# Half a pair earlier: the order of the gate sums in the output stage of an attention and feed-forward kernel

## The chip, the core and the metric

The kernel runs on one core of a Trainium2 chip. The metric is the device time of one execution in microseconds (us), as the median of several runs. A core has five engines that run side by side, each through its own instructions in a fixed order: TensorE (PE in the profile, with its weight loads as PEld), VectorE (DVE), ScalarE (ACT), GpSimd (POOL) and SyncE (SP), which here issues the transfers. An engine waits at an instruction until the semaphores that it names have been reached, and everything behind it on that engine waits as well.

## The reference

The inputs are q, k, v of shape (8, 8, 576, 64), w_in of (512, 2048) and w_out of (2048, 512). What is computed, cut to what matters:

```
attn_out = attention(q, k, v)       # 4 heads see the last 32 positions, 4 heads every 32nd one
x = attn_out.transpose(0, 2, 1, 3).reshape(4608, 512)
h = x @ w_in                        # 4608 x 2048
g = h * cos(h)
out = g @ w_out                     # 4608 x 512
```

## The kernel before

The program has two stages. In the first, which ends 486 us into the span, the attention and h = x @ w_in are made batch by batch, and h goes to a scratch array in memory. The second, the output stage, makes g and g @ w_out. It is the one that the change touches.

**Blocks and pairs.** The output stage goes through 18 blocks of 256 tokens, s0 to s17, and in each through 8 pairs, f0 to f7; a pair is 256 of the 2048 columns of h. A tile (s, f) of h is 128 partitions by 512 numbers. Products are made with numbers split in two: a high part that the fast matrix format holds, and the rest, the low part. A pair needs the high part of its gate against both parts of w_out and then the low part against the high part of w_out (`pair`, line 697). A plain pair takes 12 matmuls of 512 columns: 8 with the gate's high part, 4 with the low part. In blocks 1 to 16 the pairs f1, f3 and f5 are made with seven products in place of eight (a 2 by 2 Strassen scheme): 21 matmuls of 256 columns, 14 with the high part and 7 with the low part. For this their gates are summed first, so their tile has 896 numbers a partition rather than 512.

**The gate of one tile** (`gate`, line 631) is made in steps, each a piece of a generator:

- the load of h (`h_in`, line 634, SyncE's queue, 5 buffers);
- ScalarE turns h into a whole number of turns (line 641, into `r`, 3 buffers), and VectorE takes these off (line 642, a scalar_tensor_tensor that reads `r` and `h_in`, both in SBUF); below these two are called the count and the reduction;
- ScalarE takes the sine (`wave`, line 645, in PSUM, 3 buffers), and VectorE multiplies by h (line 652 for plain pairs, line 659 for pairs with seven products; one input is in PSUM);
- for pairs with seven products GpSimd makes the sums in three instructions (lines 660, 661, 664);
- ScalarE casts the high part (line 175), and the rest is taken off for the low part (line 176): on GpSimd, for f2 and f4 on VectorE. The buffers of `g_hi` and `g_lo` are three each.

**What sets the order.** Before each pair, `ahead` (line 674) begins one more step for the tiles that lie 2, 3, 4 and 6 pairs ahead (LEADS). From this a scheduler makes the fixed order of each engine, with estimates of its own; it also chooses which of the three buffers of `r` a tile takes. Which buffer is taken matters in the prediction: the count of f1 writes the `r` that the low part of the block before's f6 has read last.

**Around the pairs.** The outputs of a block stand in four PSUM tiles, and a fifth is free (`seats`, line 686). The tile "most" of a block is the tile "lower" of the block before it, so the first matmul into "most", the eleventh in pair f1, waits until VectorE has written that block's first half out (line 745). For the shared sums of the seven products, ScalarE copies a bank after f5 (line 730), and VectorE adds three times (lines 731, 733, 736).

**The last tiles of w_out.** Six of the 16 tiles of w_out are loaded and split only when the output stage begins (line 899, LATE). The cast is by ScalarE for three and by VectorE for the other three, and GpSimd takes the low part of all six.

Of the kernel before, what the change touches and what calls it, by code (L numbers as in the profile page):

```python
# [26 lines left out]
P = 128  # L27
# [52 lines left out]
NTB = NTOK // TB  # L80
SEVEN = (1, 3, 5)

LEADS = (6, 4, 3, 2)
AHEAD = tuple(PER_BATCH - n for n in (20, 17, 13, 10, 7, 3))

BY_VECTOR = (2, 4)
# [11 lines left out]
def attention_cos_ffn(ctx, tc, qkl, vl, qkvs, w_in, w_out, eye, eye16, mask_l0, mask_l, mask_s, out):  # L98
# [74 lines left out]

    def split(x, hi, lo, cast=nc.scalar.copy, rest=nc.gpsimd):
        with_product(cast(out=hi, in_=x))  # L175
        rest.tensor_tensor(out=lo, in0=x, in1=hi.bitcast(F32), op=ALU.subtract)  # L176

    wi, whole = [], []

# [398 lines left out]
        nc.sync.dma_start(out=w_all[n], in_=t)  # L578
        yield

    def output_weights(room, n, cast):
        both = room()
        t = wp.tile([P, 2, 2, 2 * P], F32R, name="w", bufs=2 * NF).rearrange("p l m n -> p l (m n)")
        nc.sync.dma_start(out=both, in_=w_all[n])
        yield
        split(both, t[:, 0], t[:, 1], cast)
        wo.append((t[:, 0], t[:, 1]))
        yield

# [38 lines left out]
    def seven(s, f):  # L628
        return 0 < s < NTB - 1 and f in SEVEN

    def gate(s, f):

        h = hp.tile([P, 2 * TB], F32, name="h_in")
        nc.sync.dma_start(
            out=h.rearrange("p (f t) -> p f t", f=2),
            in_=h_all[2 * f:2 * f + 2, :, s * TB:(s + 1) * TB].rearrange("f p t -> p f t"),
        )
        yield
        r = rp.tile([P, 2 * TB], F32, name="r")
        k = r.bitcast(I32)  # L640
        with_product(nc.scalar.activation(out=k, in_=h, func=AF.Copy, scale=1.0 / (2.0 * math.pi), bias=0.25))  # L641
        nc.vector.scalar_tensor_tensor(out=r, in0=k, scalar=-2.0 * math.pi, in1=h, op0=ALU.mult, op1=ALU.add)  # L642
        yield
        wave = sg.tile([P, 2 * TB], F32, name="wave")
        sin = nc.scalar.activation(out=wave, in_=r, func=AF.Sin, bias=quarter)  # L645
        with_product(sin)
        if s == 0 and f == 0:
            order(sin, exps[-1], "one change of tables")
        pool = nc.gpsimd
        if not seven(s, f):  # L650
            low, pool = (wave, nc.vector) if f in BY_VECTOR else (r, nc.gpsimd)
            nc.vector.tensor_tensor(out=low, in0=wave, in1=h, op=ALU.mult)  # L652
            yield
            g_hi, g_lo = (gp.tile([P, 7 * P], F32R, name=name) for name in ("g_hi", "g_lo"))
            split(low, g_hi[:, :4 * P], g_lo[:, :4 * P], rest=pool)
            gates[s, f] = g_hi, g_lo
            yield
        g = gs.tile([P, 8, P], F32, name="g")
        nc.vector.tensor_tensor(out=g[:, :4].rearrange("p n t -> p (n t)"), in0=wave, in1=h, op=ALU.mult)
        pool.tensor_tensor(out=g[:, 4], in0=g[:, 0], in1=g[:, 2], op=ALU.add)  # L660
        pool.tensor_tensor(  # L661
            out=g[:, 5:7], in0=g[:, 0:5:4], in1=g[:, 1:2].broadcast_to([P, 2, P]), op=ALU.subtract
        )
        pool.tensor_tensor(out=g[:, 7], in0=g[:, 3], in1=g[:, 6], op=ALU.subtract)  # L664
        yield
        g_hi, g_lo = (gp.tile([P, 7 * P], F32R, name=name) for name in ("g_hi", "g_lo"))
        split(g[:, 1:].rearrange("p n t -> p (n t)"), g_hi, g_lo)
        gates[s, f] = g_hi, g_lo
        yield

    tiles = [(s, f) for s in range(NTB) for f in range(NF)]
    work = [gate(*tile) for tile in tiles]

    def ahead(i):
        for lead in reversed(LEADS):
            if 0 <= i + lead < len(work):
                next(work[i + lead])

    class Outputs:

# [13 lines left out]
            at = self.banks[name][:, begin:end].rearrange("p n d -> p (n d)")  # L694
            in_turn(nc.tensor.matmul(at, a, w, start=first, stop=True, skip_group_check=True))  # L695

        def pair(self, f, g_hi, g_lo):

            w1, w2 = wo[2 * f:2 * f + 2]
            if seven(self.s, f):  # L700
# [59 lines left out]
    with ExitStack() as phase:  # L760
# [87 lines left out]
            in_steps(whole_output_weights(cv, n), at - 10, at)  # L848
        for n in range(NFC - LATE):
            at = (B - 1) * PER_BATCH + STEP * (n // 2) + 12 + 3 * (n % 2)  # L850
            in_steps(output_weights(lambda: whole_tile(cv)[:, :DM], n, nc.scalar.copy), at - 6, at)
        for n, f in enumerate(SEVEN):
            at = 2 * PER_BATCH + 17 * (2 * f + 2)
            in_steps(output_sums(cv, n), at, at + 8)
# [42 lines left out]
    seats = [f"q{i}" for i in range(5)]  # L897
    made = {}
    for n in range(NFC - LATE, NFC):
        cast = nc.vector.tensor_copy if n % 2 else nc.scalar.copy  # L900
        weights = output_weights(lambda: tp.tile([P, DM], F32, name="both", bufs=LATE), n, cast)
        next(weights)
        made[n + LATE - NFC] = [weights]
    for i, (s, f) in enumerate(tiles):
        if f == 0:
            block = Outputs(s)
        ahead(i)
        for step in made.get(i, ()):
# [103 lines left out]
```

## Time and profile before

| | us |
|---|---|
| median of 3 runs | 879.77 (879.46 to 881.08) |
| the profiled execution's own time | 880.64 |
| its span, first to last instruction | 878.7 |
| outside the span | 1.9 |
| TensorE busy | 866.3 (99%) |
| VectorE, ScalarE, GpSimd busy | 579.6, 516.9, 519.1 |
| mean granted TensorE clock | 0.996 |

Busy time says that an engine had an instruction in hand, not that it advanced: matmuls overlap in the pipeline, and an instruction that stands in front of a closed port counts as busy. So the prediction reads starts: how far two starts of the same kind lie apart, and what was released just before an instruction that starts late. All times in rows are us from the start of the span.

### The profile page before, as it was taken

The numbers are of one execution on the slowest core, as the hardware profiler recorded it, in microseconds if no ns is written. First come the engines' busy times: TensorE is split into PE (matmuls) and PEld (weight loads), VectorE is DVE, ScalarE is ACT, GpSimd is POOL, SyncE is SP. The second block draws the span as 40 slices with busy tenths as digits, with TensorE's granted clock in tenths as the row PEclk, the third lists the DMA queues.
The fourth block names the chain that finished last, engine by engine and source line by source line (L and its number), as shares of the span: only waits on it lengthen the run. The fifth ranks groups of instructions, "written<-read, shape, count | busy, mean of one in ns | idle before, by whom it ended". The sixth has DMA issues, their size and how long they took to land.

```text
span 878.7 us, 22516 instructions
## 1 busy us (share of the span) xinstructions
PE 866.3 (99%) x8877; PEld 790.1 (90%) x8877; DVE 579.6 (66%) x1069; ACT 516.9 (59%) x1024; POOL 519.1 (59%) x464
## 2 busy tenths in 40 slices
PE   8999999999999999999999999999999999999998
PEld 5799899999999999999999888888888888888886
DVE  5788656656667566666334667777777777777772
ACT  4676444545345354454457676777776777777772
POOL 3578974415215242261266687777777777777762
PEclk9899999999999999999999999999999999999999
DMA  9688344555856575664275643443444444443431
GB/s 339 193 286 277 133 157 159 192 190 155 295 192 209 187 259 196 226 230 146 106 246 194 192 128 120 120 120 120 121 122 124 127 122 127 124 122 120 125 118 46
DMA packets 90778, 148.63 MB, mean 169 GB/s; under 512 B 8368, under 2 KB 52912, under 8 KB 90672
## 3 DMA queue, kind: packets, MB, share of 16 engines
q1 hardware_dynamic: 89952, 146.96, 51.1%
q8 instruction: 70, 1.15, 0.6%
q14 instruction: 36, 0.29, 0.1%
q10 hardware_dynamic: 720, 0.23, 0.1%
HBM read 94.21 MB, written 52.95 MB: 167 GB/s over the span
## 4 chain that ended last, share of the span: by engine, by line
PE 54%; POOL 1%; DVE 0%; ACT 0%; issue 0%; POOLq 0%
PE q L695 43%; PE m L527 6%; PE n L527 3%; PE o L527 1%; POOL g_lo L176 0%; PE acc L328 0%; PE acc L393 0%; POOL g L661 0%; PE acc L310 0%; ACT wave L645 0%; POOL g L660 0%; DVE o L752 0%; PE acc L380 0%; ACT g_hi L175 0%; DVE r L642 0%
## 5 line engine op out<-in xcount | busy, mean ns | idle before, releaser
L695 PE MATMUL q<-w,g_hi 128*128 128x512 f32 (+1 forms) x1060 | 233.5, 360 | 0.2 <-ACT g_hi L175 0.2
L695 PEld LDWEIGHTS q<-w,g_hi 128*128 128x128 f32 x1060 | 182.2, 189 | 31.5 <-ACT g_hi L175 0.6
L642 DVE SCALAR_TENSOR_TENSOR r<-r,h_in 128x512 f32<-128x512 int32 x144 | 131.0, 926 | 42.9 <-ACT r L641 42.3
L695 PE MATMUL q<-w,g_lo 128*128 128x512 f32 (+1 forms) x530 | 129.7, 362 | 0.5 <-POOL g_lo L176 0.4
L176 POOL TENSOR_TENSOR g_lo<-g,g_hi 128x896 fp32r<-128x896 f32 x48 | 102.9, 2143 | 37.3 <-ACT g_hi L175 37.3
L645 ACT ACTIVATE wave<-r,quarter 128x512 f32<-128x512 f32 x144 | 98.4, 692 | 27.9 <-DVE r L642 26.4
L527 PE MATMUL m<-x_hi,w 128*128 128x288 f32 x448 | 109.7, 300 | 1.4 <-DVE h L545 1.0
L695 PEld LDWEIGHTS q<-w,g_lo 128*128 128x128 f32 x530 | 92.8, 189 | 18.6 <-POOL g_lo L176 3.7
L527 PE MATMUL m<-x_hi,v 128*128 128x288 f32 x448 | 108.9, 298 | 0.0
L641 ACT ACTIVATE r<-h_in 128x512 int32<-128x512 f32 x144 | 85.1, 622 | 31.7 <-POOL g_lo L176 29.7
L176 POOL TENSOR_TENSOR g_lo<-r,g_hi 128x512 fp32r<-128x512 f32 x60 | 83.4, 1403 | 18.9 <-ACT g_hi L175 15.2
L527 PEld LDWEIGHTS m<-x_hi,w 128*128 128x128 f32 x448 | 78.0, 188 | 3.0 <-DVE h L545 1.5
L535 ACT COPY m<-m 128x288 f32<-128x288 f32 x112 | 44.6, 398 | 60.7 <-PE m L527 53.2
L527 PEld LDWEIGHTS m<-x_hi,v 128*128 128x128 f32 x448 | 78.0, 188 | 1.0 <-ACT m L535 0.2
L280 POOL TENSOR_TENSOR pn_s<-e_sb,z 128x324 f32<-128x324 f32 x28 | 20.9, 747 | 88.6 <-DVE z L278 77.7
L175 ACT CAST g_hi<-g 128x896 fp32r<-128x896 f32 x48 | 45.1, 939 | 47.5 <-POOL g L664 47.5
L280 POOL TENSOR_TENSOR e_sb<-e_sb,z 128x384 f32<-128x384 f32 x24 | 20.6, 859 | 88.2 <-DVE z L278 66.3
L652 DVE TENSOR_TENSOR r<-wave,h_in 128x512 f32<-128x512 f32 x60 | 39.7, 683 | 42.0 <-ACT wave L645 42.0
L527 PE MATMUL m<-x_lo,w 128*128 128x288 f32 x224 | 66.1, 295 | 0.0
L527 PE MATMUL m<-x_lo,v 128*128 128x288 f32 x224 | 66.1, 295 | 0.0
L527 PE MATMUL n<-x_hi,v 128*128 128x288 f32 x224 | 55.1, 300 | 1.8 <-ACT n L535 1.8
L498 PE MATMUL m<-x_hi,w 128*128 128x288 f32 x256 | 55.3, 301 | 0.0
(135 smaller groups left out, 2018.3 us busy)
## 6 DMA issues: line engine op xcount, KB each, us to landing
h_all<-h SPq DMA_DIRECT2D x128, 288.0 KB, 2.7
h_in<-h_all SPq DMA_DIRECT2D x144, 256.0 KB, 2.9
qk<-in_qkvs SPq DMA_DIRECT2D x28, 324.0 KB, 3.8
out<-o SPq DMA_DIRECT2D x35, 256.0 KB, 3.0
qk<-in_qkl SPq DMA_DIRECT2D x21, 416.0 KB, 4.2
raw<-in_w_in SPq DMA_DIRECT2D x16, 512.0 KB, 4.9
raw<-in_w_out SPq DMA_DIRECT2D x16, 512.0 KB, 4.8
v<-in_vl SPq DMA_DIRECT2D x24, 224.0 KB, 3.8
```

Source lines behind the costliest of these rows:

```text
L175: with_product(cast(out=hi, in_=x))
L176: rest.tensor_tensor(out=lo, in0=x, in1=hi.bitcast(F32), op=ALU.subtract)
L280: nc.gpsimd.tensor_tensor(out=pn, in0=e, in1=z[:, :n].unsqueeze(2).broadcast_to([P, n, w]), op=ALU.mult)
L498: in_turn(nc.tensor.matmul(self.banks[i, j], a[:, c * P:(c + 1) * P], y[:, c], start=k == 0 and m == 0, stop=k == 1 and m == len(ops) - 1, ...
L527: in_turn(nc.tensor.matmul(bank, a[:, c * P:(c + 1) * P], y[:, c], start=first and i == 0, stop=i == len(ops) - 1, skip_group_check=True,))
L535: nc.scalar.copy(out=t, in_=self.bank[name[0]])
L641: with_product(nc.scalar.activation(out=k, in_=h, func=AF.Copy, scale=1.0 / (2.0 * math.pi), bias=0.25))
L642: nc.vector.scalar_tensor_tensor(out=r, in0=k, scalar=-2.0 * math.pi, in1=h, op0=ALU.mult, op1=ALU.add)
L645: sin = nc.scalar.activation(out=wave, in_=r, func=AF.Sin, bias=quarter)
L652: nc.vector.tensor_tensor(out=low, in0=wave, in1=h, op=ALU.mult)
L695: in_turn(nc.tensor.matmul(at, a, w, start=first, stop=True, skip_group_check=True))
```

## The change

Three things are changed, and the result is the same.

- The steps of pairs with seven products have leads of their own: 7, 4.5, 3.5 and 2 pairs ahead. The half steps are made in the middle of a pair, between its matmuls with the high part and those with the low part (`halfway`). Count, reduction, sine, product and sums of these pairs so come half a pair sooner in the order; the load comes a whole pair sooner, as far as the 5 buffers let it.
- GpSimd's work on gates (sums and low parts) is chained in the order in which it is written (`by_gpsimd`), and the scheduler may not change it any more.
- All six late tiles of w_out are cast by ScalarE, and the low part of every second one is taken by VectorE rather than GpSimd.

```diff
-LEADS = (6, 4, 3, 2)
+LEADS = ((6, 4, 3, 2), (7, 4.5, 3.5, 2))
...
+    of_gates = []
+
+    def by_gpsimd(begun):
+        if of_gates:
+            order(begun, of_gates[-1], "pair by pair")
+        of_gates.append(begun)
...
-            split(low, g_hi[:, :4 * P], g_lo[:, :4 * P], rest=pool)
+            lo = split(low, g_hi[:, :4 * P], g_lo[:, :4 * P], rest=pool)
+            if pool is nc.gpsimd:
+                by_gpsimd(lo)
...
-        pool.tensor_tensor(out=g[:, 4], in0=g[:, 0], in1=g[:, 2], op=ALU.add)
-        pool.tensor_tensor(
+        by_gpsimd(pool.tensor_tensor(out=g[:, 4], in0=g[:, 0], in1=g[:, 2], op=ALU.add))
+        by_gpsimd(pool.tensor_tensor(
             out=g[:, 5:7], in0=g[:, 0:5:4], in1=g[:, 1:2].broadcast_to([P, 2, P]), op=ALU.subtract
-        )
-        pool.tensor_tensor(out=g[:, 7], in0=g[:, 3], in1=g[:, 6], op=ALU.subtract)
+        ))
+        by_gpsimd(pool.tensor_tensor(out=g[:, 7], in0=g[:, 3], in1=g[:, 6], op=ALU.subtract))
...
-        split(g[:, 1:].rearrange("p n t -> p (n t)"), g_hi, g_lo)
+        by_gpsimd(split(g[:, 1:].rearrange("p n t -> p (n t)"), g_hi, g_lo))
...
-    def ahead(i):
-        for lead in reversed(LEADS):
-            if 0 <= i + lead < len(work):
-                next(work[i + lead])
+    def ahead(at):
+        for i, tile in enumerate(tiles):
+            if i - at in LEADS[seven(*tile)]:
+                next(work[i])
...
                     for w in both:
                         self.add(*to, g_hi[:, n * P:(n + 1) * P], w)
+                if group is groups[0]:
+                    halfway()
...
-        cast = nc.vector.tensor_copy if n % 2 else nc.scalar.copy
-        weights = output_weights(lambda: tp.tile([P, DM], F32, name="both", bufs=LATE), n, cast)
+        rest = nc.vector if n % 2 else nc.gpsimd
+        weights = output_weights(lambda: tp.tile([P, DM], F32, name="both", bufs=LATE), n, rest)
...
-        block.pair(f, *gates.pop((s, f)))
+        block.pair(f, *gates.pop((s, f)), partial(ahead, i + 0.5))
```

In the lists below line numbers of the changed kernel are 1 to 12 higher: 660, 661, 664 are its 670, 671, 674; 175 is 176 and 176 is 177; 641 is 649, 642 is 650; 645 is 653; 652 is 660 and 659 is 669; 731, 733, 736 are 743, 745, 748; and 745 is 757 (so 660 and 745 name other instructions there).

**GpSimd, one block.** The rows begin behind the low part of f7 of block 3 and end with the last sum of f5 of block 4. The `g_lo` that reads `r` is the low part of f0, those that read `g` are low parts of pairs with seven products; three rows on one `g` are the sums of f1, then f3, then f5. Before:

```order
L176 TENSOR_TENSOR g_lo_8864<-r_8810,g_hi_8863 128x512
L660 TENSOR_TENSOR g_8869<-g_8869 128x128
L661 TENSOR_TENSOR g_8869<-g_8869 128x256
L664 TENSOR_TENSOR g_8869<-g_8869 128x128
L176 TENSOR_TENSOR g_lo_8894<-g_8869,g_hi_8893 128x896
L660 TENSOR_TENSOR g_8929<-g_8929 128x128
L661 TENSOR_TENSOR g_8929<-g_8929 128x256
L664 TENSOR_TENSOR g_8929<-g_8929 128x128
L660 TENSOR_TENSOR g_8994<-g_8994 128x128
L661 TENSOR_TENSOR g_8994<-g_8994 128x256
L176 TENSOR_TENSOR g_lo_8954<-g_8929,g_hi_8953 128x896
L664 TENSOR_TENSOR g_8994<-g_8994 128x128
```

After:

```order
L670 TENSOR_TENSOR g_8855<-g_8855 128x128
L671 TENSOR_TENSOR g_8855<-g_8855 128x256
L674 TENSOR_TENSOR g_8855<-g_8855 128x128
L177 TENSOR_TENSOR g_lo_8871<-r_8810,g_hi_8870 128x512
L177 TENSOR_TENSOR g_lo_8899<-g_8855,g_hi_8898 128x896
L670 TENSOR_TENSOR g_8915<-g_8915 128x128
L671 TENSOR_TENSOR g_8915<-g_8915 128x256
L674 TENSOR_TENSOR g_8915<-g_8915 128x128
L177 TENSOR_TENSOR g_lo_8957<-g_8915,g_hi_8956 128x896
L670 TENSOR_TENSOR g_8983<-g_8983 128x128
L671 TENSOR_TENSOR g_8983<-g_8983 128x256
L674 TENSOR_TENSOR g_8983<-g_8983 128x128
```

The low part of f0 moved behind the sums of f1, which now follow the low part of f7 directly, and the low part of f3 moved ahead of all sums of f5 (before, two of the three stood in front of it).

**VectorE, the same stretch.** It begins with the reduction of f1 of block 4 (a row on `r` that reads `r` and `h_in`); rows on `g` and `wave` are products, rows on `t` the shared sums of block 3, and the row on `o` writes the first half of block 3 out. Before:

```order
L642 SCALAR_TENSOR_TENSOR r_8834<-r_8834,h_in_8780 128x512
L642 SCALAR_TENSOR_TENSOR r_8874<-r_8874,h_in_8813 128x512
L731 TENSOR_TENSOR t_8860<-q4_8719,t_8860 128x256
L659 TENSOR_TENSOR g_8869<-wave_8867,h_in_8780 128x512
L733 TENSOR_TENSOR t_8860<-q1_8730,t_8860 128x512
L652 TENSOR_TENSOR wave_8897<-wave_8897,h_in_8813 128x512
L642 SCALAR_TENSOR_TENSOR r_8900<-r_8900,h_in_8837 128x512
L736 TENSOR_TENSOR t_8860<-q1_8730,t_8860 128x256
L642 SCALAR_TENSOR_TENSOR r_8934<-r_8934,h_in_8877 128x512
L642 SCALAR_TENSOR_TENSOR r_8960<-r_8960,h_in_8903 128x512
L745 TENSOR_TENSOR o_8917<-q2_8693,t_8860 128x512
```

After:

```order
L650 SCALAR_TENSOR_TENSOR r_8825<-r_8825,h_in_8758 128x512
L669 TENSOR_TENSOR g_8855<-wave_8853,h_in_8758 128x512
L650 SCALAR_TENSOR_TENSOR r_8874<-r_8874,h_in_8813 128x512
L650 SCALAR_TENSOR_TENSOR r_8889<-r_8889,h_in_8815 128x512
L743 TENSOR_TENSOR t_8867<-q4_8719,t_8867 128x256
L745 TENSOR_TENSOR t_8867<-q1_8730,t_8867 128x512
L660 TENSOR_TENSOR wave_8902<-wave_8902,h_in_8813 128x512
L669 TENSOR_TENSOR g_8915<-wave_8913,h_in_8815 128x512
L748 TENSOR_TENSOR t_8867<-q1_8730,t_8867 128x256
L650 SCALAR_TENSOR_TENSOR r_8934<-r_8934,h_in_8877 128x512
L650 SCALAR_TENSOR_TENSOR r_8949<-r_8949,h_in_8879 128x512
L757 TENSOR_TENSOR o_8924<-q2_8693,t_8867 128x512
```

The product of f1 moved up, right behind its reduction, and the reductions of f2 and f3 follow it; the reductions of f4 and f5 still stand in front of `o`, but now behind the products of f2 and f3.

**ScalarE, the same stretch.** A row on `g_hi` casts a high part (here f6 and f7 of block 3, then f0 of block 4), a row on `r` counts, a row on `wave` takes a sine. Before:

```order
L175 CAST g_hi_8803<-r_8753 128x512
L645 ACTIVATE wave_8831<-r_8810,quarter_70 128x512
L175 CAST g_hi_8827<-r_8777 128x512
L641 ACTIVATE r_8834<-h_in_8780 128x512
L175 CAST g_hi_8863<-r_8810 128x512
L641 ACTIVATE r_8874<-h_in_8813 128x512
L730 COPY t_8860<-q4_8719 128x256
L645 ACTIVATE wave_8867<-r_8834,quarter_70 128x512
```

After:

```order
L176 CAST g_hi_8803<-r_8753 128x512
L653 ACTIVATE wave_8836<-r_8810,quarter_70 128x512
L649 ACTIVATE r_8825<-h_in_8758 128x512
L176 CAST g_hi_8832<-r_8779 128x512
L653 ACTIVATE wave_8853<-r_8825,quarter_70 128x512
L649 ACTIVATE r_8874<-h_in_8813 128x512
L649 ACTIVATE r_8889<-h_in_8815 128x512
L176 CAST g_hi_8870<-r_8810 128x512
```

The count of f1 (`r_8834` before, `r_8825` after) moved ahead of the cast of f7, and the sine of f1 ahead of the cast of f0.

## Rows read from the trace of the kernel before

**Rows 1.** Busy time of each engine in four stretches, each one block of the output stage (blocks 1 to 4): start and end, length, then PE, PEld, DVE, ACT and POOL busy with counts, granted clock, DMA share and GB/s.
```profile
507.61:530.80 23.19, 21.98 (x124) 18.82 (x123) 16.16 (x23) 16.62 (x29) 19.16 (x17) 1.00 0.40 122
530.80:552.29 21.49, 21.48 (x125) 18.87 (x123) 15.58 (x24) 15.20 (x26) 17.09 (x16) 1.00 0.40 123
552.29:573.77 21.48, 21.47 (x124) 18.86 (x123) 15.57 (x24) 15.17 (x26) 17.08 (x16) 1.00 0.42 123
573.77:595.25 21.48, 21.48 (x125) 18.86 (x123) 15.57 (x24) 15.15 (x26) 17.09 (x16) 1.00 0.41 123
```

**Rows 2.** The timeline of PE around block 3: start, duration of the group, matmul, count. A run of x8 on `w,g_hi` with 512 columns begins a plain pair, one of x6 with 256 columns a pair with seven products (544.31 is f5 of block 2, 560.27 is f3 of block 3).
```profile
544.31 0.88 PE L695 MATMUL q<-w,g_hi 128*128 128x256 f32 x6
545.02 1.12 PE L695 MATMUL q<-v,g_hi 128*128 128x256 f32 x8
...
546.82 2.00 PE L695 MATMUL q<-w,g_hi 128*128 128x512 f32 x8
...
560.27 0.88 PE L695 MATMUL q<-w,g_hi 128*128 128x256 f32 x6
...
562.11 0.62 PE L695 MATMUL q<-w,g_lo 128*128 128x256 f32 x3
...
563.05 2.00 PE L695 MATMUL q<-w,g_hi 128*128 128x512 f32 x8
```

**Rows 3.** Who waited for whom on PE's weight loads from 519 to 875 us, the whole answer: us in total, times, longest.
```profile
PEld q L695 <- POOL g_lo L176: 3.7, 16, 0.6
```

**Rows 4.** The timeline of POOL over one block: start, duration, line, count, and in brackets the idle time before and what ended it. The x3 are the low parts of f6 and f7 of block 2 and f0 of block 3.
```profile
544.58 4.25 POOL L176 TENSOR_TENSOR g_lo<-r,g_hi 128x512 fp32r<-128x512 f32 x3
550.39 0.47 POOL L660 TENSOR_TENSOR g<-g 128x128 f32<-128x128 f32 x1 [1.56 <-DVE g L659]
550.93 0.74 POOL L661 TENSOR_TENSOR g<-g 128x256 f32<-128x256 f32 x1
551.75 0.79 POOL L664 TENSOR_TENSOR g<-g 128x128 f32<-128x128 f32 x1
553.88 2.14 POOL L176 TENSOR_TENSOR g_lo<-g,g_hi 128x896 fp32r<-128x896 f32 x1 [1.34 <-ACT g_hi L175]
555.98 0.46 POOL L660 TENSOR_TENSOR g<-g 128x128 f32<-128x128 f32 x1
...
557.34 0.92 POOL L664 TENSOR_TENSOR g<-g 128x128 f32<-128x128 f32 x1
558.22 0.91 POOL L660 TENSOR_TENSOR g<-g 128x128 f32<-128x128 f32 x1
...
559.90 2.15 POOL L176 TENSOR_TENSOR g_lo<-g,g_hi 128x896 fp32r<-128x896 f32 x1
561.99 0.93 POOL L664 TENSOR_TENSOR g<-g 128x128 f32<-128x128 f32 x1
563.98 2.13 POOL L176 TENSOR_TENSOR g_lo<-g,g_hi 128x896 fp32r<-128x896 f32 x1 [1.05 <-ACT g_hi L175]
```

**Rows 5.** The timeline of ACT in the same block, columns as above: the count of f1, its sine, the cast of f5, the count of f1 one block later.
```profile
545.90 0.63 ACT L641 ACTIVATE r<-h_in 128x512 int32<-128x512 f32 x1 [1.63 <-POOL g_lo L176]
...
547.95 0.70 ACT L645 ACTIVATE wave<-r,quarter 128x512 f32<-128x512 f32 x1
...
562.96 0.94 ACT L175 CAST g_hi<-g 128x896 fp32r<-128x896 f32 x1 [1.48 <-POOL g L664]
...
567.39 0.63 ACT L641 ACTIVATE r<-h_in 128x512 int32<-128x512 f32 x1 [1.63 <-POOL g_lo L176]
```

**Rows 6.** The timeline of DVE in the same block: the reductions of f1 and f2, those of f4 and f5 (x2), the write of the block before's first half, the reduction of f0 of the next block.
```profile
546.57 1.10 DVE L642 SCALAR_TENSOR_TENSOR r<-r,h_in 128x512 f32<-128x512 int32 x1 [2.32 <-ACT r L641]
547.82 1.55 DVE L642 SCALAR_TENSOR_TENSOR r<-r,h_in 128x512 f32<-128x512 int32 x1 [0.15 <-ACT r L641]
...
552.47 1.28 DVE L642 SCALAR_TENSOR_TENSOR r<-r,h_in 128x512 f32<-128x512 int32 x2
553.67 0.68 DVE L745 TENSOR_TENSOR o<-q,t 128x512 f32<-128x512 f32 x1
...
561.62 0.98 DVE L642 SCALAR_TENSOR_TENSOR r<-r,h_in 128x512 f32<-128x512 int32 x1
```

**Rows 7.** Groups of DVE instructions by line and shape over the whole span: count, busy us, mean ns of one, idle before.
```profile
L642 DVE SCALAR_TENSOR_TENSOR r<-r,h_in 128x512 f32<-128x512 int32 x144 | 131.0, 926 | 42.9 <-ACT r L641 42.3
...
L175 DVE CAST w<-both 128x512 fp32r<-128x512 f32 x3 | 4.0, 1318 | 1.9 <-DMA both<-w_all 1.9
```

**Rows 8.** The timeline of all engines at the start of the output stage: low parts of late w_out tiles on POOL (494.33 and 500.25), the low parts of f6 and f7 of block 0 (501.51), the count of f1 of block 1, and two starts on PE in pair f1 of block 1.
```profile
494.33 4.52 POOL L176 TENSOR_TENSOR w<-both,w 128x512 fp32r<-128x512 f32 x3
...
500.25 1.29 POOL L176 TENSOR_TENSOR w<-both,w 128x512 fp32r<-128x512 f32 x1
...
501.51 2.99 POOL L176 TENSOR_TENSOR g_lo<-r,g_hi 128x512 fp32r<-128x512 f32 x2
...
503.28 0.63 ACT L641 ACTIVATE r<-h_in 128x512 int32<-128x512 f32 x1 [0.46 <-POOL g_lo L176]
...
510.69 0.97 PE L695 MATMUL q<-w,g_hi 128*128 128x256 f32 x6 [0.20 <-ACT g_hi L175]
...
512.79 0.74 PE L695 MATMUL q<-v,g_hi 128*128 128x256 f32 x4 [0.66 <-ACT o L752]
```

More of the change, by code (lines that the diff above doesn't have):

```diff
@@ L175, in split @@
         with_product(cast(out=hi, in_=x))
-        rest.tensor_tensor(out=lo, in0=x, in1=hi.bitcast(F32), op=ALU.subtract)
+        return rest.tensor_tensor(out=lo, in0=x, in1=hi.bitcast(F32), op=ALU.subtract)
     wi, whole = [], []
@@ L579, in whole_output_weights, with output_weights @@
         yield
-    def output_weights(room, n, cast):
+    def output_weights(room, n, rest=nc.gpsimd):
         both = room()
@@ L585, in output_weights @@
         yield
-        split(both, t[:, 0], t[:, 1], cast)
+        split(both, t[:, 0], t[:, 1], rest=rest)
         wo.append((t[:, 0], t[:, 1]))
@@ L695, in add, with pair @@
             in_turn(nc.tensor.matmul(at, a, w, start=first, stop=True, skip_group_check=True))
-        def pair(self, f, g_hi, g_lo):
+        def pair(self, f, g_hi, g_lo, halfway):
             w1, w2 = wo[2 * f:2 * f + 2]
@@ L850, in attention_cos_ffn @@
             at = (B - 1) * PER_BATCH + STEP * (n // 2) + 12 + 3 * (n % 2)
-            in_steps(output_weights(lambda: whole_tile(cv)[:, :DM], n, nc.scalar.copy), at - 6, at)
+            in_steps(output_weights(lambda: whole_tile(cv)[:, :DM], n), at - 6, at)
         for n, f in enumerate(SEVEN):
```

## The prediction

> **What bounds the kernel now.** I read the stretches first, block by block [rows 1]. TensorE is busy for all but 0.01 of the 21.49 us of a block, which hides a wait that a matmul in the pipeline covers: so I looked at starts instead. A pair with seven products lasts 546.82 - 544.31 = 2.51 us where nothing holds it up (f5) and 563.05 - 560.27 = 2.78 at f3, because its low-part matmuls begin only at 562.11 [rows 2]. The waits of the weight loads name GpSimd's low part, 16 times, once in each block with seven products [rows 3]. So TensorE's own pace is 21.49 - 0.27 = 21.22 us a block, and 0.27 us a block is lost.
>
> GpSimd is not busy all the time either (17.1 of 21.5 us) [rows 1]. What closes the circle is a chain through four engines that returns to itself one block later. I set a clock to zero where the low part of f6 ends, which is when ScalarE's count of f1 starts, 545.90; that count had waited for it, because it writes the buffer of `r` that this low part reads [rows 5]. Then, by [rows 4]: sums of f1 from 4.49; low part of f1 from 7.98, after 1.34 us idle for its cast; sums of f3 from 10.08; first two sums of f5 from 12.32; low part of f3 from 14.00; last sum of f5; 1.05 idle for the cast; low part of f5 from 18.08; low part of f6, and the next count at 567.39, which is 21.49 [rows 5]. The circle is 0.27 longer than TensorE's pace, and that is the wait.
>
> **A price that the circle pays.** VectorE's reduction takes 0.68 us where GpSimd is idle (two in 1.28 at 552.47) [rows 6]. At 561.62 it meets the low part of f3, which ends at 562.05, and the reduction ends at 562.60, 0.55 later [rows 4, 6]. GpSimd's next sum, begun at 561.99, takes 0.93; the sums of 128 columns take 0.46 to 0.47 where nothing is in their way [rows 4]. So the two exclude each other: the reduction stands until GpSimd's instruction in hand is done, then GpSimd's next one stands some 0.45 us. VectorE's other work shows none of this: 0.68 at 553.67 [rows 6], though GpSimd is busy from 553.88 [rows 4]. The circle pays four times: 0.33, 0.46, 0.45 and 0.47 (the sums at 551.75, 557.34, 558.22, 561.99) [rows 4], 1.7 us. Bare, it is 19.8.
>
> The Trainium skill, page "SBUF — State Buffer", section "Who interferes with whom", says that a VectorE instruction with two SBUF inputs and a GpSimd instruction that reads SBUF exclude each other for the whole instruction. By that rule the sum at 561.99 would have ended at 562.60 + 0.46 = 563.06; it ended at 562.92 [rows 4], so it loses 0.13 less than the rule has it. By the rule the seven meetings below would cost 0.9 us a block more and the forecast would be about 902; I go by the row.
>
> **The change, part 1: the new circle.** Same clock, durations of [rows 4 to 6], hand-overs of 0.03 to 0.08 as in these rows; the order is that of the lists.
> - Count of f1 0.63, reduction 0.68, sine 0.70, product 0.68: sums of f1 from 2.89, not 4.49. The product now follows its reduction at once, and GpSimd is idle meanwhile, since the cast of f7 stands behind the count of f1 now: low part of f7 from 1.25 to 2.54.
> - Sums of f1: 0.46 + 0.74 + 0.46 and two hand-overs, 1.80 bare. The reductions of f2 and f3, now behind the product of f1, come at 2.8 and 3.4, right among them: 0.43 and 0.35. End 5.48.
> - Low part of f0, moved here, to 6.8. It hides the cast of f1, which ends at 6.7.
> - The reduction of f4 comes at 6.7, just before the low part of f0 ends, and is through at 7.39. The low part of f1 starts 0.4 late and ends at 9.35 to 9.39.
> - The reduction of f5 comes at 7.3 and stands until 9.94. Before, f4's and f5's ran in the 1.34 us in which GpSimd was idle, at 552.47 [rows 4, 6]. Sums of f3, 0.4 late: end 11.6.
> - Cast of f3: 1.05 with hand-overs, not hidden any more (the first sums of f5 used to lie over it). Low part of f3, 12.65 to 14.78.
> - On ScalarE the counts of f6 and f7 stand behind that cast, so their reductions come at 13.1 and after: they meet the low part of f3 and the sums of f5, 0.4 and 0.35. Sums end at 17.34. Cast 1.05, low part of f5 18.39 to 20.52.
> - The reduction of f0 meets that low part, and the low part of f6 loses 0.37: it ends at 22.23.
>
> Sum: 2.89 + 2.59 + 1.32 + 2.59 + 2.21 + 1.05 + 2.13 + 2.56 + 1.05 + 2.13 + 1.71 = 22.23. Bare that is 19.5, 0.3 less than before, but it meets the reduction seven times (2.7 us) rather than four (1.7).
>
> A circle of 22.23 against 21.22 makes TensorE wait 1.0 us a block, and the place is new. The write of the block before's first half stands on VectorE behind the reduction of f5: it runs from 9.86 to 10.54. TensorE needs that bank for the eleventh matmul of f1, 0.71 (545.02 - 544.31) for six and half of that and a little more for four, 1.2 into the pair [rows 2]; f0 in front of it takes (21.22 - 3 x 2.51) / 5 = 2.74, so that is 3.9 into the block. So a block can't start before 10.54 - 3.9 = 6.6 on this clock. The low part of f3 (14.78; needed behind 14 of the 21 matmuls of f3, 2.74 + 2.51 + 2.74 + 1.67 = 9.7 into the block) would allow 5.1: the wait that the change is aimed at goes, and the bank is late in its place. Queued behind the reduction of f5 stand also the product of f4 and the low part of f2; both have over 1 us left.
>
> Blocks 2 to 16, 15 waits: 15 x (22.23 - 21.49) = +11.1.
>
> **Part 2: the start.** Block 1 takes 23.19 us [rows 1], 1.97 over TensorE's pace: it waits for the cast of f1, then 0.66 for a bank [rows 8]. GpSimd takes low parts of late w_out tiles in front of the low parts of f5 and f6: three of these six go. At 1.29 each that is up to 3.9 us; the casts of f5 and f6 don't come that much sooner, and I take 2.8 (between 0 and 3.9, nearer to the upper end, since the lone one at 500.25 stands right before the low part of f6): its end moves from 503.28 to 500.5 [rows 8]. On the clock, block 1 then starts at 507.61 - 500.5 = 7.1, later than the 6.6 needed: no wait, -1.97, and the 0.5 left is used up before the first wait, -0.5. ScalarE gets three casts more, VectorE loses three of 1.32 [rows 7] and gets three low parts. No row shows VectorE at such a low part: 0.68 by the row at 553.67, 1.32 by the cast [rows 6, 7]; I take the lower, beside idle time either way.
>
> The same section of the Trainium skill would have these three stand for GpSimd's instructions too, since both inputs lie in SBUF; no run here shows it, and it would move only the 2.8.
>
> **Sum.** 11.1 - 1.97 - 0.5 = +8.6 on the profiled execution's 880.64, 889.2. That execution was 0.87 over the median: **888.4 us**, +1.0%.
>
> **Rivals.** One tenth of a microsecond decides whether a reduction meets GpSimd or slips by, and each meeting is worth 0.33 to 0.47 a block.
> - *The change does what it is for.* GpSimd runs ahead of TensorE instead of behind, pauses for buffers, and the reductions fall into its pauses as f4's and f5's did at 552.47 [rows 6]. Then the bare circle (19.5) is under 21.22 even with three or four meetings, and TensorE never waits: -1.97 - 15 x 0.27 = -6.0, 873.8, **faster**. For it: the start gives GpSimd 2.8 us. Against: only 0.5 us of that is left over in block 1, and the meetings follow from the order of the queues, which is the same in each block. Decides if four or fewer of the seven meetings stay on the circle.
> - *Two meetings fewer*: circle 21.4, as before; only the start is won, about 877.5.
> - *One fewer*: 21.8, 15 x 0.3 - 2.5 = +2.1, 882.
> - *Worse than forecast*: each meeting at 0.47, or a second place late, circle 22.5: about 893.
>
> **Chances and range.** The forecast, with 0.2 us a block either way (885 to 892): 0.60. One fewer 0.11; two fewer 0.12; runs free 0.12; worse 0.05. Below 877 lie the free case and a part of the two-fewer case, above 893 half of the worst: the range is 877 to 893. The forecast's own range is 885 to 892. A median of this kernel can be told from 879.77 by about 0.2%, 1.8 us. Faster: the free case and most of two fewer, 0.19; same: the rest of it and a little of one fewer, 0.06; slower 0.75.
>
> **What would show it.** In the profile after: blocks 2 to 16 at 22.2 us each and block 1 at 21.2; the wait for GpSimd's low part at f3 gone, and in its place about 15 waits of 1.0 us in f1, released by VectorE's write of `o`; the reduction's mean up from 926 ns [rows 7] to about 1,250, that of f5 at 2.6 us; GpSimd's low parts of 896 columns at f1 at 2.5 us. It is wrong if the reduction's mean stays near 0.93, or if blocks take 21.2 to 21.5.

## The result, and the profile after

The changed kernel takes 888.12 us (median of 4 runs, 887.43 to 888.88), the kernel before 879.62 us on the same chip: ratio 1.009, 95% interval 1.0077 to 1.0104. It is slower by 0.9%, and the forecast was 888.4. The profiled execution took 888.88 us with a span of 887.0; before these were 880.64 and 878.7.

The first view is again the busy time by stretch, blocks 1 to 4 of the changed kernel, columns as in [rows 1]:

```profile
508.04:529.25 21.21, 21.21 (x124) 18.82 (x123) 16.77 (x20) 14.58 (x25) 17.08 (x14) 1.00 0.41 121
529.25:552.74 23.49, 21.76 (x124) 18.79 (x123) 19.92 (x26) 16.58 (x28) 19.22 (x18) 1.00 0.39 116
552.74:574.77 22.03, 21.48 (x124) 18.87 (x123) 18.47 (x24) 15.13 (x26) 17.84 (x16) 1.00 0.40 120
574.77:596.81 22.04, 21.48 (x124) 18.86 (x123) 18.47 (x24) 15.12 (x26) 17.85 (x16) 1.00 0.39 120
```

Against [rows 1]: block 1 lost its 1.98 us of waiting, block 2 is 2.00 longer, and each later block is 0.55 longer. The busy time of VectorE in a steady block rose from 15.57 to 18.47 though it has the same 24 instructions: some of them stand longer. GpSimd's rose by 0.76.

Who waited for whom from 519 to 875 us (total, times, longest), all engines, cut to the rows on TensorE. The 16 waits of [rows 3] for GpSimd's low parts are gone but for one, which is at f0 of block 2:

```profile
PEld q L705 <- DVE o L757: 12.7, 15, 1.9
...
PE q L705 <- DVE o L757: 9.7, 15, 1.7
...
PEld q L705 <- POOL g_lo L177: 0.4, 1, 0.4
```

PE's timeline shows the place, the eleventh matmul of f1: in block 2 the long wait, in block 3 the usual one. Four matmuls on `v` start late, behind the write of the block before's first half:

```profile
535.34 0.74 PE L705 MATMUL q<-v,g_hi 128*128 128x256 f32 x4 [1.73 <-DVE o L757]
...
555.46 0.88 PE L705 MATMUL q<-w,g_hi 128*128 128x256 f32 x6
556.17 0.64 PE L705 MATMUL q<-v,g_hi 128*128 128x256 f32 x4
557.37 0.74 PE L705 MATMUL q<-v,g_hi 128*128 128x256 f32 x4 [0.55 <-DVE o L757]
```

GpSimd's timeline, to be laid beside [rows 4]: the low part of f6 at the start of the stage, then a steady block from one low part of f6 to the next (544.69 and 566.71 are low parts of f6; the sums of f1 begin at 549.36, of f3 at 555.26, of f5 at 560.98).

```profile
499.73 1.30 POOL L177 TENSOR_TENSOR g_lo<-r,g_hi 128x512 fp32r<-128x512 f32 x1 [0.76 <-ACT g_hi L176]
...
544.69 1.74 POOL L177 TENSOR_TENSOR g_lo<-r,g_hi 128x512 fp32r<-128x512 f32 x1
...
549.36 0.91 POOL L670 TENSOR_TENSOR g<-g 128x128 f32<-128x128 f32 x1 [0.37 <-DVE g L669]
550.34 1.07 POOL L671 TENSOR_TENSOR g<-g 128x256 f32<-128x256 f32 x1
...
551.91 1.30 POOL L177 TENSOR_TENSOR g_lo<-r,g_hi 128x512 fp32r<-128x512 f32 x1
553.18 2.12 POOL L177 TENSOR_TENSOR g_lo<-g,g_hi 128x896 fp32r<-128x896 f32 x1
555.26 0.91 POOL L670 TENSOR_TENSOR g<-g 128x128 f32<-128x128 f32 x1
556.24 1.05 POOL L671 TENSOR_TENSOR g<-g 128x256 f32<-128x256 f32 x1
...
558.89 2.13 POOL L177 TENSOR_TENSOR g_lo<-g,g_hi 128x896 fp32r<-128x896 f32 x1 [1.05 <-ACT g_hi L176]
560.98 0.91 POOL L670 TENSOR_TENSOR g<-g 128x128 f32<-128x128 f32 x1
561.97 1.07 POOL L671 TENSOR_TENSOR g<-g 128x256 f32<-128x256 f32 x1
...
564.63 2.13 POOL L177 TENSOR_TENSOR g_lo<-g,g_hi 128x896 fp32r<-128x896 f32 x1 [1.05 <-ACT g_hi L176]
566.71 1.75 POOL L177 TENSOR_TENSOR g_lo<-r,g_hi 128x512 fp32r<-128x512 f32 x1
```

Seven of these instructions are longer than their bare time (0.46, 0.74 and 1.29): two at each of the three sums, and the low part of f6. They lose 0.45, 0.33, 0.45, 0.31, 0.45, 0.33 and 0.46, together 2.8 us of the 22.02 from 544.69 to 566.71. Each such loss is called a meeting below. VectorE's timeline has the other side, columns as in [rows 6]: first a reduction at the start of the stage (f0 of block 1), then, in the steady block, the reductions of f2 and f3, those of f4 and f5, then the write `o`, those of f6 and f7, and that of f0. Two reductions in one row (x2) take 1.28 where GpSimd is idle, one takes 0.68.

```profile
500.16 1.41 DVE L650 SCALAR_TENSOR_TENSOR r<-r,h_in 128x512 f32<-128x512 int32 x1 [0.30 <-ACT r L649]
...
549.25 1.56 DVE L650 SCALAR_TENSOR_TENSOR r<-r,h_in 128x512 f32<-128x512 int32 x2
...
553.38 3.33 DVE L650 SCALAR_TENSOR_TENSOR r<-r,h_in 128x512 f32<-128x512 int32 x2
556.63 0.68 DVE L757 TENSOR_TENSOR o<-q,t 128x512 f32<-128x512 f32 x1
...
559.63 2.81 DVE L650 SCALAR_TENSOR_TENSOR r<-r,h_in 128x512 f32<-128x512 int32 x2
...
565.78 1.53 DVE L650 SCALAR_TENSOR_TENSOR r<-r,h_in 128x512 f32<-128x512 int32 x1
```

How such rows are read: the reduction of f4 begins at 553.38, just behind the begin of the low part of f1 (553.18), stands until that ends at 555.30, and goes ahead of GpSimd's next sum, which takes 0.91 rather than 0.46. The reduction of f5 then stands in front of that sum until 556.17, and ends 0.54 later, at 556.71. Only then can `o` be written.

The groups over the whole span, which answer to [rows 7], and GpSimd's sums (L670, L671 and L674 are the first, second and third of a pair):

```profile
L650 DVE SCALAR_TENSOR_TENSOR r<-r,h_in 128x512 f32<-128x512 int32 x144 | 175.1, 1244 | 8.3 <-ACT r L649 7.4
...
L671 POOL TENSOR_TENSOR g<-g 128x256 f32<-128x256 f32 x48 | 50.8, 1058 | 3.8
...
L670 POOL TENSOR_TENSOR g<-g 128x128 f32<-128x128 f32 x48 | 43.6, 909 | 5.9 <-DVE g L669 5.9
...
L674 POOL TENSOR_TENSOR g<-g 128x128 f32<-128x128 f32 x48 | 22.3, 464 | 3.8
```

### The profile page after: what moved, and what is told of

The parts are those of the page before. It is cut to its first block, busy times and chain, and to the rows that moved or that the text cites. A ratio compares the mean times of both kernels' runs of the same rounds, so it can differ in the third digit from the quotient of the medians.

```text
span 887.0 us, 22471 instructions
## 1 busy us (share of the span) xinstructions
PE 865.0 (98%) x8877; PEld 790.2 (89%) x8877; DVE 627.1 (71%) x1069; ACT 517.3 (58%) x1027; POOL 526.9 (59%) x461
## 4 chain that ended last, share of the span: by engine, by line
PE 35%; DVE 10%; issue 6%; ACT 3%; POOL 3%; DVEq 0%; POOLq 0%
PE q L705 23%; PE m L528 6%; DVE r L650 5%; PE n L528 3%; POOL g_lo L177 3%; ACT r L649 2%; PE o L528 1%; ACT wave L653 1%; DVE t L745 1%; DVE o L757 1%; DVE g L669 1%; DVE t L743 1%; DVE t L748 1%; PE acc L329 0%; PE acc L394 0%
## 5 line engine op out<-in xcount | busy, mean ns | idle before, releaser
L650 DVE SCALAR_TENSOR_TENSOR r<-r,h_in 128x512 f32<-128x512 int32 x144 | 175.1, 1244 | 8.3 <-ACT r L649 7.4
L528 PE MATMUL m<-x_hi,w 128*128 128x288 f32 x448 | 109.7, 300 | 1.4 <-DVE h L546 1.0
L177 POOL TENSOR_TENSOR g_lo<-r,g_hi 128x512 fp32r<-128x512 f32 x60 | 85.7, 1429 | 38.8 <-ACT g_hi L176 37.1
L705 PE MATMUL q<-v,g_hi 128*128 128x256 f32 x384 | 57.8, 287 | 9.7 <-DVE o L757 9.7
L705 PEld LDWEIGHTS q<-v,g_hi 128*128 128x128 f32 x384 | 50.3, 191 | 12.7 <-DVE o L757 12.7
```

The costliest lines, as they stand in the source:

```text
L177: return rest.tensor_tensor(out=lo, in0=x, in1=hi.bitcast(F32), op=ALU.subtract)
L528: in_turn(nc.tensor.matmul(bank, a[:, c * P:(c + 1) * P], y[:, c], start=first and i == 0, stop=i == len(ops) - 1, skip_group_check=True,))
```

## The experiments

**Theory.** A circle through ScalarE, VectorE and GpSimd takes 22.04 us a block, TensorE needs 21.22, and what lengthens the circle are the meetings of VectorE's reduction (both inputs in SBUF) with GpSimd. **Rivals.** The chain on GpSimd lays the cast of f3 bare and that costs; the bank behind VectorE's queue costs, whatever the circle; part 2 costs.

Times below are medians; before was run on the same chip each time (880.48 for e1 to e4, 880.23 for e5 to e8, 880.30 for e9 to e12). The ratios are those on record, which are not the plain quotients of the medians. A block is the distance of two starts of f1 in the timeline of PE in the steady part; the mean of the reduction is from the groups by line.

| run | kernel | us | ratio to before (95%) | block, us | mean reduction, ns |
|---|---|---|---|---|---|
| | before | | 1 | 21.48 | 926 |
| | after | 888.12 | 1.0090 (1.0077 to 1.0104) | 22.04 | 1244 |
| e1 | part 2 alone | 889.53 | 1.0106 (1.0089 to 1.0123) | 22.13 | 1138 |
| e2 | chain and part 2, old leads | 893.24 | 1.0140 (1.0125 to 1.0155) | 22.45 | 1051 |
| e3 | after, count in PSUM | 874.46 | 0.9927 (0.9912 to 0.9941) | 21.22 | 682 |
| e4 | before, count in PSUM | 874.63 | 0.9930 (0.9916 to 0.9945) | 21.22 | 681 |
| e5 | as e3, but in an SBUF tile | 896.36 | 1.0176 (1.0159 to 1.0193) | 22.74 | 1345 |
| e6 | after without part 2 | 895.72 | 1.0175 (1.0160 to 1.0190) | 22.47 | 838 |
| e7 | after, bank first | 892.52 | 1.0136 (1.0121 to 1.0151) | 21.8 to 23.4, at the end 22.47 | 1020 |
| e8 | e1, count in PSUM | 874.60 | 0.9940 (0.9924 to 0.9955) | 21.22 | 681 |
| e9 | after, f0 alone in PSUM | 880.87 | 1.0003 (0.9992 to 1.0013) | 21.61 | 1204 and 680 |
| e10 | after, f5 alone in PSUM | 883.30 | 1.0023 (1.0005 to 1.0042) | 21.74 | 1279 and 678 |
| e11 | after, f0 and f4 in PSUM | 874.60 | 0.9933 (0.9912 to 0.9955) | 21.22 | 1182 and 681 |
| e12 | e2, count in PSUM | 874.25 | 0.9936 (0.9917 to 0.9955) | 21.22 | 684 |

**e3: the count in PSUM.** The tile `wave` is taken one step sooner and holds the count, so that the reduction has one input in PSUM. GpSimd's rows stay as they were; VectorE's and ScalarE's are in another order.

```diff
         r = rp.tile([P, 2 * TB], F32, name="r")
-        k = r.bitcast(I32)
+        wave = sg.tile([P, 2 * TB], F32, name="wave")
+        k = wave.bitcast(I32)
...
         yield
-        wave = sg.tile([P, 2 * TB], F32, name="wave")
         sin = nc.scalar.activation(out=wave, in_=r, func=AF.Sin, bias=quarter)
```

> The changed kernel with one change: the count writes into the PSUM tile wave rather than into r, so that the reduction reads one input from PSUM and one from SBUF; GpSimd's order stays the same row for row. Theory (reduction and GpSimd exclude each other only while the reduction has both inputs in SBUF, and these meetings make the circle 22.05): reduction at 0.68 us wherever GpSimd is, mean about 0.7 instead of 1.24, sums of 128 columns at 0.47, no waits of TensorE for o, blocks of 21.22 us, 888.1 - 15 x 0.83 = about 875.6. Rival A (GpSimd's order and the bank behind the queue of VectorE make the circle, ports or not): 886 to 888, waits for o stay. Rival B (the reduction is dear for its form): its mean stays over 1.1, 888.

874.46. The groups over its span: the reduction costs what it costs with GpSimd idle, and no sum on GpSimd loses anything.

```profile
L651 DVE SCALAR_TENSOR_TENSOR r<-wave,h_in 128x512 f32<-128x512 int32 x144 | 95.5, 682 | 29.5 <-issue 22.5 <-POOL g_lo L177 4.7 <-ACT wave L650 2.2
...
L671 POOL TENSOR_TENSOR g<-g 128x256 f32<-128x256 f32 x48 | 35.5, 740 | 3.8
L674 POOL TENSOR_TENSOR g<-g 128x128 f32<-128x128 f32 x48 | 22.1, 461 | 3.8
L670 POOL TENSOR_TENSOR g<-g 128x128 f32<-128x128 f32 x48 | 22.1, 461 | 0.0
```

TensorE waits for nothing from 500 to 875 us. Two blocks of it by stretch, block 1 and a later one, both at TensorE's own pace:

```profile
506.42:527.64 21.22, 21.22 (x125) 18.81 (x123) 13.62 (x23) 15.54 (x27) 15.65 (x17) 1.00 0.42 125
570.08:591.30 21.22, 21.22 (x125) 18.81 (x123) 13.96 (x24) 15.06 (x26) 15.08 (x16) 1.00 0.40 124
```

The Trainium skill, page "SBUF — State Buffer", section "Who interferes with whom", says that a VectorE instruction with at most one SBUF input, outside the 2-port performance modes, does not contend with GpSimd; these rows agree (682 ns beside a GpSimd that is busy 15 of 21 us).

**e5: its control.** e3 also frees the count from waiting for a buffer of `r` and moves rows. So the count was given a tile of its own in SBUF, and the rows of GpSimd, VectorE and ScalarE in a steady block are those of e3:

```diff
         r = rp.tile([P, 2 * TB], F32, name="r")
-        k = r.bitcast(I32)
+        k = rp.tile([P, 2 * TB], I32, name="k", bufs=2)
```

> The control of e3: the count writes a tile k of its own in SBUF (two buffers), so that it waits for no buffer of r, as in e3, and the rows of GpSimd, VectorE and ScalarE in a block are those of e3; only the reduction has both inputs in SBUF again. Theory (what e3 takes away is the meeting of two SBUF readers): the mean of the reduction stays over 1.1 us, sums of GpSimd lose about 0.45 us again, and the time is well above e3, 881 to 889. Rival (what e3 takes away is the wait of the count for the buffer of r, or it is the new order on VectorE): the time of e3, 874.5.

896.36, above the range that was named, and 22 us above e3. The rows of the three engines are those of e3, in the same order, up to the last block, and in neither run does ScalarE wait ahead of the count (0.0 us idle): only where the count lies differs. The rival falls. One line of its groups is enough:

```profile
L650 DVE SCALAR_TENSOR_TENSOR r<-k,h_in 128x512 f32<-128x512 int32 x144 | 190.8, 1345 | 5.1 <-issue 4.8 <-ACT k L649 0.3
```

**e4: the kernel before with the count in PSUM** (the diff of e3).

> The kernel before with the count in PSUM, as in the run ahead. Theory (before, too, four meetings stood on the circle): mean of the reduction about 0.7 instead of 0.93, 16 waits of 0.2 to 0.3 us for the low part of f3 gone, blocks 2 to 16 at 21.22, 879.6 - 15 x 0.27 = about 875.5. Rival (the four meetings cost nothing, the wait for the low part of f3 comes from the order of GpSimd alone): 879.6.

874.63, no waits, every block at 21.22, block 1 too: nothing is left of the 0.27 a block and the 1.97 of block 1. That meetings made these waits is not shown by this run alone. With GpSimd not chained, the scheduler also gives GpSimd another order here, in the steady blocks that of e1 below, and the count no longer waits for a buffer of `r`; no control like e5 was run on this kernel. What is shown with e1 is that the same rows on GpSimd go with blocks of 22.13 us when both inputs lie in SBUF and of 21.22 when one lies in PSUM.

**e9 to e11: single meetings.** The diff of e3 for some pairs only (`early = f in (0,)`, `(5,)`, `(0, 4)`). In the steady blocks all rows keep their order, so that each run takes away named meetings and nothing else.

> The changed kernel with the count in PSUM for the tiles of f0 alone; the rows of GpSimd and VectorE stay in the same order. Theory (the circle of 22.04 is 19.3 bare and seven meetings of 0.31 to 0.45, each of which counts by itself): the reduction of f0 no longer makes the low part of f6 lose 0.45 (1.74 to 1.29), circle 21.59, waits for o 15 x 0.4, time 888.1 - 15 x 0.45 = 881.4. Rival A (the meeting only moves to another place on the circle): 886 to 888. Rival B (the bank behind the reduction of f5 is the cause): 888.

880.87. The rows of GpSimd's low part of f6, one block apart: 1.29 rather than 1.75, and 21.60 from one to the next.

```profile
585.96 1.29 POOL L177 TENSOR_TENSOR g_lo<-r,g_hi 128x512 fp32r<-128x512 f32 x1
...
607.56 1.30 POOL L177 TENSOR_TENSOR g_lo<-r,g_hi 128x512 fp32r<-128x512 f32 x1
```

> The changed kernel with the count in PSUM for the tiles of f5 alone, whose reduction stands right ahead of the write that TensorE waits for. Theory (one meeting fewer, at the second sum of f3, 1.05 to 0.74): circle 21.73, time 888.1 - 15 x 0.31 = 883.5, and waits for o stay. Rival (the bank that waits behind this reduction is the cause): waits for o gone, 875.6.

883.30, and 15 waits for `o` remain. The same row, and the second sum of f3, which lost its 0.31 (1.05 before this edit): a circle of 21.75.

```profile
586.51 1.75 POOL L177 TENSOR_TENSOR g_lo<-r,g_hi 128x512 fp32r<-128x512 f32 x1
...
598.07 0.74 POOL L675 TENSOR_TENSOR g<-g 128x256 f32<-128x256 f32 x1
...
608.26 1.75 POOL L177 TENSOR_TENSOR g_lo<-r,g_hi 128x512 fp32r<-128x512 f32 x1
```

> The changed kernel with the count in PSUM for the tiles of f0 and f4. Theory (two meetings of 0.45 fewer): circle 21.14, under TensorE's own 21.22, so the waits are gone but for the first blocks and the time is near that with no meeting at all, 874.5 to 877. Rival A (meetings move, they don't add up): 882 or more. Rival B (all seven are needed): 881.4 as with f0 alone.

874.60, without any wait of TensorE. With f4 out of the way the reduction of f5 meets the first sum of f3 in its place (0.92) and the second goes free (0.74), so what falls away is 0.46 + 0.31 rather than twice 0.45. GpSimd's low part of f6, the two sums, and the low part of f6 fourteen blocks after the first:

```profile
541.82 1.29 POOL L177 TENSOR_TENSOR g_lo<-r,g_hi 128x512 fp32r<-128x512 f32 x1
...
594.51 0.92 POOL L674 TENSOR_TENSOR g<-g 128x128 f32<-128x128 f32 x1
595.50 0.74 POOL L675 TENSOR_TENSOR g<-g 128x256 f32<-128x256 f32 x1
...
839.71 1.30 POOL L177 TENSOR_TENSOR g_lo<-r,g_hi 128x512 fp32r<-128x512 f32 x1
```

From 541.82 to 839.71 that is 21.28 a block, 0.06 more than TensorE takes. GpSimd falls behind by under 1 us in the whole stage, which its lead at the start covers.

**e1: part 2 alone,** on the kernel before.

```diff
...
-        cast = nc.vector.tensor_copy if n % 2 else nc.scalar.copy
-        weights = output_weights(lambda: tp.tile([P, DM], F32, name="both", bufs=LATE), n, cast)
+        rest = nc.vector if n % 2 else nc.gpsimd
+        weights = output_weights(lambda: tp.tile([P, DM], F32, name="both", bufs=LATE), n, rest)
```

> The kernel before with part 2 of the change alone (all six late w_out tiles cast by ScalarE, every second low part by VectorE); leads and GpSimd's chain stay as before. Theory (part 2 gives back what block 1 waits for, 1.97 us, and a little of the first circle; the circle of later blocks is a matter of its own): about 877.3 if later blocks stay at 21.49 us. Rival A (the start is no matter, since the next blocks wait longer): 879.6. Rival B (once GpSimd has a lead it runs free): 873.8. The scheduler also puts the low part of f0 between the sums of f1 here, so a circle a few tenths off 21.49 is possible, each tenth 1.5 us.

889.53, beyond every case that was named. With GpSimd not chained, the scheduler answers this edit at the start with another order in all later blocks (the low part of f0 between the sums of f1), and TensorE waits 15 times for `o`.

**e8: e1 with the count in PSUM.**

> The kernel of e1 (before with part 2 alone, 889.5) with the count in PSUM. Theory (what e1 lost it lost to meetings, since the scheduler's new order put more of them on the circle): reduction at 0.68, no waits for o, TensorE at its own pace and block 1 without its wait of 1.97: 872.5 to 874.6. Rival (the order of e1, with the low part of f0 between the sums of f1, is itself too long): 885 or more.

874.60. The loss of e1 is gone to the last microsecond, with the same rows on GpSimd. Nothing is left of part 2's gain either: e4, without it, has 874.63. Here and in e12 VectorE's and ScalarE's rows change with the edit, as they do in e3; the control for that, e5, was run on the changed kernel only.

**e2 and e12: chain and part 2 with the old leads,** alone and with the count in PSUM.

```diff
-LEADS = ((6, 4, 3, 2), (7, 4.5, 3.5, 2))
+LEADS = ((6, 4, 3, 2), (6, 4, 3, 2))
```

> The changed kernel with the leads of the kernel before (6, 4, 3, 2 for all pairs): chain on GpSimd and part 2 stay. Theory (the circle counts, and what the chain does to it is to lay the cast of f3 bare that the first sums of f5 used to cover): the circle is about 0.5 us longer than before, 22.0, so 15 x 0.5 - 2.5 on 879.6, about 884.6. Rival A (the half pair is what costs, the chain is free): 877. Rival B (the chain is the whole cost): 888.

893.24, well above the 884.6 of the theory and the 888 of rival B. The new leads are no loss by themselves: beside this kernel the changed one is 5 us faster.

> The kernel of e2 (chain and part 2, leads as before, blocks of 22.44) with the count in PSUM. Theory (meetings are what makes it slow too, the bare cast of f3 adds about 0.5 to a bare circle that is over 1 us shorter than TensorE's pace): blocks of 21.22, 874 to 875.6. Rival (the cast of f3 laid bare is what costs): 880 or more, with waits for g_lo of f3.

874.25. The bare cast of f3 costs nothing as long as the circle stays under 21.22.

**e6: the changed kernel without part 2** (the reverse of e1's diff).

> The changed kernel with the last tiles of w_out as in the kernel before (three casts by VectorE, all six low parts by GpSimd). Theory (the first circle starts when GpSimd is through with them, and 15 circles of 22.05 follow): 0.5 to 2.8 us above the changed kernel, 888.6 to 890.9. Rival A (part 2 is what costs, as e1 could be read): 880 or less. Rival B (no matter): 888.1. The scheduler's rows in a steady block put the write of the first half ahead of the reduction of f5 here, so that the wait may come at another place.

895.72, a miss: 5 us above the range. The scheduler's rows on VectorE are others here too, and TensorE waits for GpSimd's low parts.

**e7: bank first.** The reductions of f4 and f5 are ordered behind the write `o`.

```diff
...
+        if f in (4, 5) and s - 1 in written:
+            order(reduced, written[s - 1], "bank first")
```

> The changed kernel with the reductions of f4 and f5 ordered behind the write of the block before's first half, so that the bank of TensorE's eleventh matmul of f1 no longer waits behind the reduction that GpSimd holds up. Theory (the circle through GpSimd, ScalarE and VectorE is what is 22 us long, the bank only the place where TensorE feels it): the waits for o in f1 go and others come, for g_hi or g_lo, 884 to 890. Rival (the queue on VectorE ahead of the write is the cause): no waits, blocks at 21.22, 875.6.

892.52. The waits for `o` go, others come, for `g_lo`, and the time rises by 4 us over the changed kernel, more than the theory's range allowed. The bank is not the cause. Its blocks differ, 21.8 to 23.4 us; in the last three VectorE has the order of e6, and they take e6's 22.47. GpSimd's timeline in e6 shows that order (low parts of f6 and f7, the first sum of f1, the low part of f1):

```profile
614.25 2.55 POOL L177 TENSOR_TENSOR g_lo<-r,g_hi 128x512 fp32r<-128x512 f32 x2
619.09 0.84 POOL L670 TENSOR_TENSOR g<-g 128x128 f32<-128x128 f32 x1 [2.29 <-DVE g L669]
...
622.95 2.68 POOL L177 TENSOR_TENSOR g_lo<-g,g_hi 128x896 fp32r<-128x896 f32 x1
```

The low parts of f6 and f7 meet nothing, but the sums of f1 then wait 2.29 us for their product, which stands behind other rows on VectorE: from the start of f6's low part to the first sum it is 4.84 us, against 4.67 in the changed kernel. The low part of f1 loses 0.55. In the whole block six rows of GpSimd lose 0.38, 0.45, 0.55, 0.45, 0.33 and 0.45, together 2.6 of 22.46 us, so that the bare circle is about 19.9, against 19.2 in the changed kernel. By this sum the extra 0.4 a block is order and not meetings. Neither kernel was run with the count in PSUM, so whether its blocks would fall to 21.22 is not shown.

## Why the prediction was right, and where it was not

- **What bounds the kernel.** TensorE's own pace of 21.22 us a block was read from single pairs; e3, e4, e8, e11 and e12 run at it.
- **The price of a meeting.** 0.33 to 0.47 was read from four rows of before; in the changed kernel the seven cost 0.31 to 0.46, and taking one away gave back 0.43 (e9) and 0.30 (e10) a block. The remark that a sum loses 0.13 less than the whole of the reduction holds too: the reduction of f4 ends at about 555.85 (0.55 behind the low part of f1), and the sum of 0.46 that was held up ends at 556.17, not 556.31.
- **The new circle.** Forecast 22.23, measured 22.03; seven meetings as forecast, one of them in another place. From row to row on GpSimd the terms are 2.93, 2.55, 1.27, **2.08**, **2.58**, 1.05, 2.09, 2.60, 1.05, 2.08 and 1.75, against 2.89, 2.59, 1.32, **2.59**, **2.21**, 1.05, 2.13, 2.56, 1.05, 2.13 and 1.71. Two were mis-sized. The reduction of f4 was to slip in just ahead of the low part of f1; it came 0.2 too late, so that low part lost nothing (2.12, not 2.5), and the sums of f3 met two reductions in place of one. For the same reason one of the named signs failed: the reduction of f5 was to stand 2.6 us and took 0.94, and that of f4 stood 2.46 (the row of 553.38 taken apart).
- **The place and number of the waits.** 15, at the eleventh matmul of f1, behind `o` and the reduction of f5, as forecast; in size 0.82 us of each steady block (22.04 - 21.22) rather than 1.0.
- **The start.** Block 1 without its wait: forecast -1.97, measured -1.98. The step that failed is the 2.8 us that the first circle was to start sooner. The low part of f6 did end 2.25 sooner (501.03 against 503.28), but the count of f1 began only at 502.23, 1.05 sooner: on ScalarE it stands behind a sine, and this waited for the reduction at 500.16, which stood 1.41 behind a low part on GpSimd. ScalarE's timeline:

```profile
501.60 0.69 ACT L653 ACTIVATE wave<-r,quarter 128x512 f32<-128x512 f32 x1 [1.48 <-DVE r L650]
502.23 0.61 ACT L649 ACTIVATE r<-h_in 128x512 int32<-128x512 f32 x1
```

  So block 2 paid 2.27 us (23.49 - 21.22) where 0.5 was forecast, some 0.3 of it at f0, for a low part of GpSimd, and the rest for `o`. The low parts of w_out that moved to VectorE were also mis-sized: two of the three met GpSimd and took 1.48 and 1.19 us, where the prediction went by 0.68 for each, and GpSimd's own low part of w_out at 493.43 took 1.75 rather than 1.29. On VectorE:

```profile
492.54 1.48 DVE L177 TENSOR_TENSOR w<-both,w 128x512 fp32r<-128x512 f32 x1 [0.37 <-ACT w L176]
...
494.54 1.19 DVE L177 TENSOR_TENSOR w<-both,w 128x512 fp32r<-128x512 f32 x1
...
499.18 0.68 DVE L177 TENSOR_TENSOR w<-both,w 128x512 fp32r<-128x512 f32 x1
```

- **The sum.** From the start of block 1 to the end the profiled execution is 7.87 us longer (378.96 against 371.09); the other 0.43 is in the first stage, which ends that much later. Forecast were 8.6: 1.8 too little for block 2, 14 x 0.19 = 2.7 too much for the later blocks, which gives 7.7. The time came out within 0.3 us because two errors of size largely cancelled and the first stage took up part of what was left. So close a hit is luck: over the profiles of all kernels here the output stage starts anywhere from 484.6 to 487.1 us.
- **The rivals.** "Two meetings fewer" and "one fewer" were priced at 877.5 and 882. With one fewer (e9, e10) it is 880.9 and 883.3. With two fewer (e11) it is 874.6, since the circle then falls to TensorE's pace and no wait is left.
- **Part 2 as a matter of the start.** The prediction let it act on block 1 and the lead into block 2 alone. Added to the kernel before (e1) or taken from the changed one (e6), it also changes the rows of the later blocks, on GpSimd in e1 and on VectorE in both, and the time by 9 and 8 us.

## What to carry to other kernels

Before moving work about, ask what makes the engine that is late so slow: here four versions of the kernel (before, after, e1, e2), at 879.6 to 893.2 us, met at 874.3 to 874.6 once the reduction had one input in PSUM, 0.7% under the kernel before and 1.5% under the changed one (e4, e3, e8, e12). That it is the place of the input, and not the order that came with it, is shown on the changed kernel (e3 against e5). Where VectorE with two SBUF inputs and GpSimd run beside each other on a closed circle, count the meetings and add them to the bare circle; only the part above the bound engine's own pace costs time. An edit at the start of a scheduled program may reorder all that follows, so a part is priced together with the rows it leaves behind.

## What the runs showed of the hardware

- An instruction of VectorE that stands in front of GpSimd's does not slow the one in hand: the low part of 896 columns took 2.12 us with a reduction standing in front of it all the while; in e3, where none stands, such low parts take 2.13 on average.
- What GpSimd's next instruction loses to a standing reduction went with its start and not with its length: 0.45 to 0.46 for a sum of 0.46 us, a low part of 1.29 and one of 2.13 (508.96 in block 1, 2.58), which all begin 0.04 to 0.05 before the end of the row ahead, and 0.31 to 0.33 for the second sums of 0.74, which begin 0.07 behind it.
- A second standing instruction is not let through with the first: of the two reductions from 553.38, the second waited for one more GpSimd instruction (3.33 us for two that take 1.28).
- ScalarE wrote whole numbers to PSUM, and VectorE read them there, at no extra cost: the count took 587 ns on average rather than 624, the reduction 682.
